# Turning an MLP's results back on VectorE, storing them piece by piece, and dealing out the loads of later pairs: top-k attention and a low-rank mixer on one core

## The chip, the cores and the metric

The kernel runs on one core of a Trainium2 chip. The core has five engines with queues of their own: TensorE (PE: matmuls and transposes, into PSUM), VectorE (DVE), ScalarE (ACT), GpSimd (POOL) and SyncE (SP), which computes nothing and here issues nearly all DMAs. Each engine runs its own instructions strictly in the order in which the kernel wrote them; between engines, semaphores hold back what needs another's result. A DMA is issued by a queue and carried out by 16 DMA engines; the issuing queue goes on to its next instruction when the issue is done, but if that instruction has to wait, all that stands behind it waits too.

The metric is the time of one execution in microseconds (us), lower is better. All data is float32 (the weights arrive as float64, read as pairs of 32-bit words).

## What is computed

```python
# attention: q, k, v are (8, 8, 576, 64): batch, heads, rows, width
scores = (1 / sqrt(64)) * q @ k.transpose(0, 1, 3, 2)
kth = np.partition(scores, -32, axis=-1)[..., -32:-31]
scores = np.where(scores >= kth, scores, -1e9)
attn = np.exp(scores - scores.max(-1, keepdims=True))
attn = attn / (attn.sum(-1, keepdims=True) + 1e-9)
x = (attn @ v).transpose(0, 2, 1, 3).reshape(8, 576, 512)
# mixer: U (576, 32), V (32, 576), w_ch1 (512, 2048), w_ch2 (2048, 512)
h = x.transpose(0, 2, 1) @ U @ V
u = x + h.transpose(0, 2, 1)
out = u + np.maximum(u @ w_ch1, 0) @ w_ch2
```

For each of 64 heads and each of 576 rows the 32 largest scores are kept, weighed and multiplied with v. The mixer joins the heads of a batch, adds a product of rank 32 along the rows, and ends with an MLP whose result is added to its input.

## The kernel before

**Pairs, steps, batches.** Two heads make a pair (`g`, 32 of them), four pairs a batch (`NPAIR` = 4). A pair is worked off in five steps (`CH`): four tiles of 128 rows, both heads side by side, and a last tile `t` = 4 with the 64 rows that are left of both heads. The main loop (L782) runs over `n` = 5 g + t. It is software-pipelined by hand: in step n the scores of tile n+1 are computed, the top-k of tile n runs, tile n-1 is weighed, turned and sent away, and tile n-3 is multiplied with v. The order of all five engines is the order of this text; no scheduler moves anything.

**A tile.** `scores` (L313) multiplies q and k on TensorE, ScalarE copies the result to SBUF (L351). From pair 5 on (`blocked`) the top-k works on folded rows: GpSimd and VectorE split each row into the larger and the smaller of two halves (`pair`, L390 to L393), and VectorE finds the 32nd largest score by `max` and `match_replace` (`front`, L432 to L463). ScalarE and GpSimd push down what is below it (L488, L491), ScalarE takes the exponential (L397). VectorE is needed in every tile for the whole of the top-k.

**Weights to the other side.** The product with v needs the weights transposed. From step 30 on (`ROUNDED`, `shared`) the four large tiles of a pair go round through DRAM: VectorE transposes blocks of 32 x 32 into `y`, which has one buffer (`blocks`, L518), SyncE stores it in four DMAs to `away` (L524) and loads it again as `PT` in one (L528), which first has to wait for those four. `values` (L585) multiplies PT with v, a little more than one step later. The fifth tile, and all before step 30, are transposed on TensorE (`turns`).

**Loads.** `load(g)` brings q, k and v of pair g. A blocked pair takes 16 DMAs of q and k in pieces of 32 columns (L247 with 64 KB, L252 with 8 KB), then five of v (L276 to L280). All 21 are written one after the other at the beginning of step t = 0 of the pair in front (L786), to be turned by VectorE (`prep`, L293) in step t = 1. The tile `ld` has one buffer; the tiles of v have three.

**The MLP as filler.** When a batch's four pairs are mixed (`mixed`), `mlp(b)` is added to `fillers`: a generator that writes one matmul at a time. `fill` is called several times in a step and takes as many of them as are `due`. A batch's MLP runs in two parts: 320 columns (two tiles and the last 64 rows), then 256. In each, 16 tiles of the hidden layer (L656, then ReLU, L668) are followed by four result tiles `c` (L675, 16 matmuls each). A finished result is copied by ScalarE (L690), and GpSimd adds u (L691, into `oT`, two buffers); in the last batch VectorE does both (L688).

**The way out.** `oT` holds the result with its columns on the partitions and must be turned back. In batches 0 to 6, `turned_back` does it on TensorE: two or three transposes (L723), one or two copies by ScalarE (L725, L727) into `ob` (two buffers), and one or two stores (L729, L734). This is written some matmuls behind the result: at f = 12 of the next result tile (L682), at f = 4 of the next part (L669), or at the end of the MLP (L694). In the last batch, but for its very last tile, VectorE turns blocks of 32 x 32 (L705), and eight or twelve stores of 16 or 8 KB follow at once (L710, L715).

Of the kernel before, what the change touches and what calls it, by code (L numbers as in the profile page):

```python
# [26 lines left out]
def kernel(  # L27
# [28 lines left out]
    nc = tc.nc  # L56
# [179 lines left out]
    inverted = set()  # L236

    def load(g):
        b, h0 = g // NPAIR, 2 * (g % NPAIR)
        ld = loads.tile([P, 2 * S], F32, tag="ld", name="ld")  # L240
        if blocked(g):
            for i, src in enumerate((q, k)):
                for a in range(4):
                    ds = src[b, h0 + a // 2, :, a % 2 * BLK : (a % 2 + 1) * BLK]
                    to = ld[a * BLK : (a + 1) * BLK, i * S : (i + 1) * S]
                    lead = TAIL if i and a >= 2 else 0
                    nc.sync.dma_start(  # L247
                        to[:, lead : lead + MAIN].rearrange("i (t m d) -> i t m d", t=NT, d=BLK),
                        ds[0:MAIN].rearrange("(m i t) d -> i t m d", i=BLK, t=NT),
                    )  # L250
                    end = 0 if lead else MAIN
                    nc.sync.dma_start(  # L252
                        to[:, end : end + TAIL].rearrange("i (m d) -> i m d", d=BLK),
                        ds[MAIN:S].rearrange("(m i) d -> i m d", i=BLK),
                    )
            raw[g] = ld
        else:
            tiles = []
            ends = ld[:, 2 * MAIN : 2 * S].rearrange("p (h d) -> p h d", h=2)
            for j, src in enumerate((q, k)):  # L260
                t = ld[:, j * MAIN : (j + 1) * MAIN].rearrange("p (t h d) -> p t h d", t=NT, h=2)
                for i in range(2):
                    queue = nc.scalar if g == 0 and i else nc.sync
                    queue.dma_start(
                        t[:, :, i, :],
                        src[b, h0 + i, 0:MAIN, :].rearrange("(p t) d -> p t d", t=NT),
                    )
                tiles.append(t)
            for i, src in enumerate((q, k)):
                nc.sync.dma_start(  # L270
                    ends[half(i)], src[b, h0 : h0 + 2, MAIN:S, :].rearrange("h p d -> p h d")
                )
            raw[g] = tiles, ends
        va, vd, vt = (a[g % NV] for a in (vas, vds, vts))
        for i in range(2):
            nc.sync.dma_start(  # L276
                va[:, i], v[b, h0 + i, 0:MAIN, :].rearrange("(p t) d -> p t d", t=NT)
            )
            nc.sync.dma_start(vd[half(i), half(i)], v[b, h0 + i, MAIN:S, :])
        nc.sync.dma_start(vt[TAIL:P], v[b, h0 : h0 + 2, MAIN:S, :].rearrange("h p d -> p h d"))  # L280

    def blocked(g):
# [363 lines left out]
    def mlp(b):  # L646

        uT = uTs.pop(b)
        late = []
        for chunks, (lo, hi) in zip(PARTS, SPAN):  # L650
            w = hi - lo
            hTs = []
            for f in range(NF):
                ph = ps_m.tile([P, C], F32, tag="mm", name="mm")
                for cc in range(NC):
                    nc.tensor.matmul(  # L656
                        ph[:, 0:w],
                        lhsT=w1[:, cc, f * P : (f + 1) * P],
                        rhs=uT[:, cc, lo:hi],
                        start=(cc == 0),  # L660
                        stop=(cc == NC - 1),
                    )
                    if cc < NC - 1:
                        yield w / C
                if f % 2 == 0:
                    hT = mlpp.tile([P, 2, WIDE], F32, tag="hT", name="hT", bufs=HT)
                    hTs += [hT[:, 0], hT[:, 1]]
                nc.scalar.activation(hTs[f][:, 0:w], ph[:, 0:w], AF.Relu)  # L668
                if f == 4 and late:  # L669
                    late.pop()()  # L670
                yield w / C
            for c in range(NC):
                po = ps_m.tile([P, C], F32, tag="mm", name="mm")
                for f in range(NF):
                    nc.tensor.matmul(  # L675
                        po[:, 0:w],
                        lhsT=w2[:, f, c * P : (c + 1) * P],
                        rhs=hTs[f][:, 0:w],
                        start=(f == 0),
                        stop=(f == NF - 1),  # L680
                    )
                    if f == 12 and late:  # L682
                        late.pop()()
                    if f < NF - 1:
                        yield w / C
                oT = mlpp.tile([P, WIDE], F32, tag="oT", name="oT")
                if b == B - 1:
                    nc.vector.tensor_tensor(oT[:, 0:w], uT[:, c, lo:hi], po[:, 0:w], ALU.add)  # L688
                else:
                    nc.scalar.copy(oT[:, 0:w], po[:, 0:w])  # L690
                    nc.gpsimd.tensor_tensor(oT[:, 0:w], oT[:, 0:w], uT[:, c, lo:hi], ALU.add)  # L691
                late.append(turned_back(b, chunks, lo, c, oT))
                yield w / C
        late.pop()()  # L694

    def turned_back(b, chunks, lo, c, oT):


        def run():
            cs = slice(c * P, (c + 1) * P)  # L700
            if b == B - 1 and (lo, c) != (SPAN[1][0], NC - 1):

                w = sum(rows(t) for t in chunks)
                ob = mlpp.tile([P, 3 * P], F32, tag="ob", name="ob", bufs=2)
                nc.vector.transpose(ob[:, 0:w], oT[:, 0:w])  # L705
                for a in range(4):
                    cs = slice(c * P + a * BLK, c * P + (a + 1) * BLK)
                    ba = ob[a * BLK : (a + 1) * BLK]
                    for t in chunks[0:2]:
                        nc.sync.dma_start(  # L710
                            out[b, 0:MAIN, cs].rearrange("(m i t) c -> t i m c", i=BLK, t=NT)[t],
                            ba[:, OFF[t] - lo : OFF[t] - lo + P].rearrange("i (m c) -> i m c", c=BLK),
                        )
                    if NT in chunks:
                        nc.sync.dma_start(  # L715
                            out[b, MAIN:S, cs].rearrange("(m i) c -> i m c", i=BLK),
                            ba[:, 2 * P : 2 * P + TAIL].rearrange("i (m c) -> i m c", c=BLK),
                        )
                return
            tp = ps_t.tile([P, 3, P], F32, tag="tp", name="tp")  # L720
            for i, t in enumerate(chunks):
                n = rows(t)
                nc.tensor.transpose(tp[0:n, i, :], oT[:, OFF[t] - lo : OFF[t] - lo + n], ident)  # L723
            ob = mlpp.tile([P, 3, P], F32, tag="ob", name="ob", bufs=2)
            nc.scalar.copy(ob[:, 0:2], tp[:, 0:2, :])  # L725
            if NT in chunks:
                nc.scalar.copy(ob[0:TAIL, 2], tp[0:TAIL, 2, :])  # L727
            t = chunks[0]
            nc.sync.dma_start(  # L729
                out[b, 0:MAIN, cs].rearrange("(p t) c -> p t c", t=NT)[:, t : t + 2, :],  # L730
                ob[:, 0:2],
            )
            if NT in chunks:
                nc.sync.dma_start(out[b, MAIN:S, cs], ob[0:TAIL, 2])  # L734

        return run

    MLP_WORK = 2 * NF * NC * S / C

# [5 lines left out]
    share = MLP_WORK / (NPAIR * SLOTS * (NT + SHORT))  # L745
    fillers, mixing, due = [], [], 0.0

    def fill(k=1):


        nonlocal due
        for _ in range(k):
            if passes:
                passes.pop(0)()
            if mixing and next(mixing[0], True):
                mixing.pop(0)
            due += share * (SHORT if t == NT else 1) * (EARLY if n <= 2 * ALONE + 2 else 1)
            while due > 0:
                if not fillers:
                    due = 0.0  # L760
                    break
                done = next(fillers[0], None)
                if done is None:
                    fillers.pop(0)
                else:
                    due -= done
# [4 lines left out]
        if m % CH == NT:  # L771
            mixing.append(mixed(m // CH, 5, 1 if m < STEPS - 1 else 0))

    load(0)
    next_params(1)
    t = 0
    for _ in prep(0):
# [4 lines left out]
    for n in range(STEPS + 2):  # L782
        g, t = divmod(n, CH)
        if n < STEPS:
            if t == 0 and g + 1 < NP:
                load(g + 1)  # L786
            if t == 1 and g + 1 < NP:
                ready = prep(g + 1)
            fronts[n] = front(g, t)
            next(fronts[n])  # L790
# [107 lines left out]
        fill(2)  # L898
    while mixing or fillers:
        fill()  # L900


# [29 lines left out]
```

## Time and profile before

Three runs took 1718.66, 1716.7 and 1718.15 us: a median of 1718.15. The profiled execution took 1716.65 us, and its span, from the first instruction to the last, is 1714.9 us.

| Engine | busy us | share of the span | instructions |
|---|---|---|---|
| TensorE, matmuls | 1613.5 | 94% | 9489 |
| TensorE, weight loads | 1219.8 | 71% | 9489 |
| VectorE | 1484.2 | 87% | 4317 |
| ScalarE | 1023.3 | 60% | 2582 |
| GpSimd | 944.9 | 55% | 749 |

| Group | number | mean of one |
|---|---|---|
| L723 transposes on TensorE | 142 | 276 ns (128 rows), 272 ns (64) |
| L725 and L727 copies by ScalarE | 57 and 28 | 372 and 258 ns |
| L691 additions by GpSimd, 320 and 256 columns | 28 and 28 | 868 and 731 ns |
| L705 block transposes on VectorE, 320 and 256 columns | 4 and 3 | 512 and 445 ns |
| L518 block transposes of the weights on VectorE | 208 | 682 ns |
| L524 stores to `away` | 416 | 434 ns to issue (median), 2.4 us to land |
| L528 loads of PT | 104 | 338 ns to issue, 3.3 us to land |
| L247 and L252 loads of q and k | 216 each | about 590 and 625 ns to issue, 2.4 and 2.0 us to land |
| L710 stores of pieces in the last batch | 56 | 430 ns to issue, 1.5 us to land |

Matmuls overlap in TensorE, so the mean duration of one is not its price: the chain of waits shows how fast they follow each other (0.11 us for a transpose, 0.22 us for each of the two records that a matmul of 256 columns leaves, 0.27 us for 320). The share of busy time is an average over stages: until 200 us attention runs without an MLP, at 1550 us attention is over, and the rest is the last MLP on TensorE alone. The granted clock is 0.97 over the span, and 1.00 from 440 us on but for the last bit. A DMA's issue occupies SyncE's queue and is not counted as busy. "A <- B" in a list of waits says that A stood until B was done.

### The profile page before, as it was taken

To read this page: it belongs to the slowest core of one execution; us is meant where nothing else is said; L and a number is where in the kernel's file an instruction comes from. 1 tells how busy PE (TensorE), PEld (TensorE's weight loads), DVE (VectorE), ACT (ScalarE), POOL (GpSimd) and SP (SyncE) were. 2 spreads that over 40 slices of the span, in tenths; PEclk is the share of its full clock that TensorE was granted. 3 is DMA by queue.
4 is the path that set the end of the run, shared out by engine and by line. 5 is a ranking of instruction groups with operands and counts; after the bars stand their busy time and mean duration, and the time that the engine had idled before them with its cause. 6 is when DMAs were issued, how large, how long until landed. Compare 5 with 4: busy or idle time off the path is not lost.

```text
span 1714.9 us, 29637 instructions
## 1 busy us (share of the span) xinstructions
PE 1613.5 (94%) x9489; PEld 1219.8 (71%) x9489; DVE 1484.2 (87%) x4317; ACT 1023.3 (60%) x2582; POOL 944.9 (55%) x749
## 2 busy tenths in 40 slices
PE   4666799998999999999999999999999999999999
PEld 2444566787777877788677877788677877788777
DVE  7999989999999999999999999999999999992000
ACT  4888797665656556565656566565655566563100
POOL 4778578666555555565555555565555555552000
PEclk7777899999999999999999999999999999999999
DMA  3322322344444444444444444444444444432010
GB/s 87 95 84 84 84 78 61 77 123 122 108 112 112 117 117 106 112 116 114 115 109 111 119 112 108 114 113 114 111 108 120 118 108 114 106 93 71 3 16 13
DMA packets 275837, 167.37 MB, mean 98 GB/s; under 512 B 173920, under 2 KB 260192, under 8 KB 275680
## 3 DMA queue, kind: packets, MB, share of 16 engines
q1 hardware_dynamic: 274624, 165.20, 37.2%
q8 instruction: 75, 1.23, 0.3%
q14 instruction: 82, 0.67, 0.1%
q10 hardware_dynamic: 1056, 0.26, 0.1%
HBM read 101.42 MB, written 63.96 MB: 96 GB/s over the span
## 4 chain that ended last, share of the span: by engine, by line
PE 71%; DVE 19%; SPq 3%; ACT 2%; issue 2%; DMA 2%; POOL 1%; POOLq 0%; DVEq 0%; ACTq 0%
PE mm L656 27%; PE mm L675 21%; PE sc L323 8%; DVE upper L458 6%; PE O L585 6%; DVE m L463 6%; DVE first L446 2%; SPq L252 2%; PE tp L551 1%; PE O L571 1%; SPq L247 1%; PE up L631 1%; PE O L581 1%; PE tp L546 1%; DVE y L518 1%
## 5 line engine op out<-in xcount | busy, mean ns | idle before, releaser
L675 PE MATMUL mm<-hT,w 128*128 128x256 f32 (+1 forms) x2048 | 529.5, 407 | 0.0
L656 PE MATMUL mm<-uT,w 128*128 128x256 f32 (+1 forms) x2048 | 522.8, 407 | 0.0
L491 POOL TENSOR_TENSOR Ssb<-Ssb,E 128x576 f32<-128x576 f32 x271 | 379.2, 1417 | 246.2 <-ACT E L488 245.8
L656 PEld LDWEIGHTS mm<-uT,w 128*128 128x128 f32 x2048 | 380.0, 191 | 97.6 <-issue 2.6
L675 PEld LDWEIGHTS mm<-hT,w 128*128 128x128 f32 x2048 | 377.9, 191 | 93.0 <-issue 2.9
L463 DVE MAX8 m<-upper 128x8 f32<-128x304 f32 (+1 forms) x864 | 407.7, 508 | 3.6
L458 DVE MATCH_REPLACE8 upper<-m,upper 128x304 f32<-128x304 f32 (+1 forms) x576 | 285.7, 502 | 0.0
L390 POOL TENSOR_TENSOR lower<-Ssb 128x576 uint32<-128x576 uint32 (+1 forms) x135 | 174.3, 1291 | 147.2 <-ACT Ssb L351 51.0
L393 POOL TENSOR_TENSOR lower<-lower,upper 128x576 uint32<-128x576 uint32 (+1 forms) x135 | 174.3, 1291 | 112.2 <-DVE upper L392 104.7
L397 ACT ACTIVATE Ssb<-Ssb,nmax 128x576 f32<-128x576 f32 x286 | 221.5, 777 | 15.3 <-POOL Ssb L468 9.3
L668 ACT ACTIVATE hT<-mm 128x320 f32<-128x320 f32 (+1 forms) x256 | 105.1, 410 | 192.9 <-PE mm L656 191.0
L323 PE MATMUL sc<-qkT 64*128 64x288 f32 x1334 | 211.7, 441 | 8.6 <-ACT Ssb L358 7.8
L488 ACT ACTIVATE E<-Ssb,least 128x576 f32<-128x576 f32 x271 | 198.0, 769 | 5.2
L323 PEld LDWEIGHTS sc<-qkT 64*128 64x128 f32 x1334 | 116.3, 183 | 63.8 <-issue 24.2
L585 PE MATMUL O<-PT,va 128*64 128x128 f32 x2048 | 144.5, 285 | 3.3 <-DMA PT<-away 3.2
L518 DVE STREAM_TRANSPOSE y<-Ssb 128x512 f32<-128x512 f32 x208 | 134.5, 682 | 14.8 <-ACT Ssb L397 14.7
L351 ACT COPY Ssb<-sc 128x576 f32<-128x576 f32 x216 | 127.5, 643 | 32.6 <-PE sc L323 31.0
L688 DVE TENSOR_TENSOR oT<-uT,mm 128x320 f32<-128x320 f32 (+1 forms) x8 | 3.6, 454 | 144.5 <-PE mm L675 144.5
L585 PEld LDWEIGHTS O<-PT,va 128*64 128x64 f32 x2048 | 113.2, 140 | 19.7 <-DMA PT<-away 3.9
L432 DVE MAX8 upper<-lower 128x8 f32<-128x288 f32 x243 | 97.9, 439 | 23.2 <-POOL lower L393 21.2
L392 DVE TENSOR_TENSOR upper<-sc,Ssb 128x576 f32<-128x576 f32 (+1 forms) x135 | 92.0, 682 | 20.7 <-ACT Ssb L351 20.1
L458 DVE MATCH_REPLACE8 upper<-first,upper 128x304 f32<-128x304 f32 x243 | 109.8, 458 | 0.0
(91 smaller groups left out, 1878.7 us busy)
## 6 DMA issues: line engine op xcount, KB each, us to landing
away<-y SPq DMA_DIRECT2D x416, 128.0 KB, 2.4
PT<-away SPq DMA_DIRECT2D x104, 512.0 KB, 3.3
raw<-in_moe_w_ch_dram SPq DMA_DIRECT2D x32, 512.0 KB, 3.9
va<-in_v_dram SPq DMA_DIRECT2D x64, 128.0 KB, 2.2
out_dram<-ob SPq DMA_DIRECT2D x57, 128.0 KB, 2.0
ld<-in_q_dram SPq DMA_DIRECT2D x108, 64.0 KB, 2.6
ld<-in_k_dram SPq DMA_DIRECT2D x108, 64.0 KB, 2.3
ld<-in_q_dram SPq DMA_DIRECT2D x108, 8.0 KB, 2.2
```

The lines of the kernel that those rows point to most:

```text
L323: nc.tensor.matmul(out, lhsT=qkT[half(h), 0, cols(t)], rhs=qkT[half(h), 1, lo:hi], start=True, stop=True,)
L390: nc.gpsimd.tensor_tensor(bottom, a.bitcast(U32), b.bitcast(U32), ALU.add)
L393: nc.gpsimd.tensor_tensor(bottom, bottom, top.bitcast(U32), ALU.subtract)
L397: nc.scalar.activation(E, chunk, AF.Exp, bias=nmax, scale=SCALE, accum_out=total)
L458: nc.vector.match_replace(nxt, ms[c], curs[c], NEG)
L463: nc.vector.max(ms[c], curs[c])
L488: nc.scalar.activation(gap, chunks[c], AF.Relu, bias=least[:, c : c + 1], scale=-WIDEN)
L491: nc.gpsimd.tensor_tensor(chunks[c], chunks[c], gap, ALU.subtract)
L518: nc.vector.transpose(y[:, :, h].rearrange("p r c j -> p c r j"), E2[:, a : a + MAIN].rearrange("p (c r j) -> p c r j", c=NT, r=4),)
L585: nc.tensor.matmul(O[half(h)], lhsT=va[:, h, j, :], rhs=PB[:, h, j] if shared(g, t) else PT[:, NT * h + j], start=False, stop=(j == NT - 1),)
L656: nc.tensor.matmul(ph[:, 0:w], lhsT=w1[:, cc, f * P : (f + 1) * P], rhs=uT[:, cc, lo:hi], start=(cc == 0), stop=(cc == NC - 1),)
L675: nc.tensor.matmul(po[:, 0:w], lhsT=w2[:, f, c * P : (c + 1) * P], rhs=hTs[f][:, 0:w], start=(f == 0), stop=(f == NF - 1),)
```

## The change

Three things change.

1. The result tiles of all batches but the very last tile are turned by VectorE and leave in pieces of 32 columns. `turn_back` is no longer written at a place in the MLP's loop but by a post: `later(6, ...)` puts it on a list with the count of MLP matmuls (`ticks`) at which it is due, and `tick()`, called after every MLP matmul, writes at most one due post.
2. In batches 0 to 6 each piece's store is a post of its own, due 1, 2, 3, ... matmuls after the transpose: twelve for the wider part (eight of 16 KB, four of 8 KB), eight for the other. In the last batch they are written at once, as before.
3. `load` becomes a generator with a `yield` behind each DMA but the last. Up to pair 5 it is run through at step t = 0 of the pair in front, as before. From pair 6 on it is started two pairs ahead, in step t = 2 (`coming`), and every `fill` writes one DMA of it; what is left is written in step t = 1, before `prep`.

```diff
-                if f == 4 and late:
-                    late.pop()()
...
-                    if f == 12 and late:
-                        late.pop()()
+                    tick()
...
-                late.append(turned_back(b, chunks, lo, c, oT))
+                later(6, lambda a=(b, chunks, lo, c, oT): turn_back(*a))
...
+    def turn_back(b, chunks, lo, c, oT):
+        cs = slice(c * P, (c + 1) * P)
+        if (b, lo, c) != (B - 1, SPAN[1][0], NC - 1):
+            w = sum(rows(t) for t in chunks)
+            ob = mlpp.tile([P, 3 * P], F32, tag="ob", name="ob", bufs=2)
+            nc.vector.transpose(ob[:, 0:w], oT[:, 0:w])
+            wait = 0
+            for a in range(4):
...
+                for to, piece in pieces:
+                    if b == B - 1:
+                        nc.sync.dma_start(to, piece)
+                    else:
+                        wait += 1
+                        later(wait, lambda to=to, piece=piece: nc.sync.dma_start(to, piece))
+            return
...
+    posts, ticks = [], 0
+    def later(wait, job):
+        at = ticks + wait
+        i = sum(p[0] <= at for p in posts)
+        posts.insert(i, (at, job))
+    def tick():
+        nonlocal ticks
+        ticks += 1
+        if posts and posts[0][0] <= ticks:
+            posts.pop(0)[1]()
+    coming = []
+    def send():
+        if coming and next(coming[0], True):
+            coming.pop(0)
     def fill(k=1):
...
             if passes:
                 passes.pop(0)()
+            send()
...
-            if t == 0 and g + 1 < NP:
-                load(g + 1)
+            if t == 0 and g <= NPAIR:
+                for _ in load(g + 1):
+                    pass
+            if t == 2 and NPAIR <= g < NP - 2:
+                coming.append(load(g + 2))
             if t == 1 and g + 1 < NP:
+                while coming:
+                    send()
                 ready = prep(g + 1)
...
     while mixing or fillers:
         fill()
+    while posts:
+        tick()
```

## The prediction

> **What bounds the kernel now.** I read first the busy time by stretch (columns: stretch, its length, then busy us and instructions of TensorE, its weight loads, VectorE, ScalarE, GpSimd, then clock, DMA share, GB/s):
>
> ```profile
> 300.00:440.00 140.00, 133.69 (x839) 104.99 (x838) 134.88 (x418) 86.36 (x225) 84.18 (x67) 0.98 0.42 106
> ...
> 700.00:800.00 100.00, 100.00 (x616) 79.71 (x615) 95.75 (x292) 60.40 (x161) 58.12 (x46) 1.00 0.44 114
> 800.00:900.00 100.00, 98.73 (x578) 72.05 (x576) 94.21 (x289) 61.38 (x154) 57.26 (x46) 1.00 0.45 114
> ```
>
> From about 440 to 1550 us TensorE is never idle but for one wait that returns in each batch, VectorE stands 4 to 6 us per 100 behind it, and after 1556 TensorE works alone at the last MLP. The chain of waits agrees: 71% TensorE, 19% VectorE. The wait that returns, and who sits on SyncE's queue, are in the waits (us in total, times, longest):
>
> ```profile
> PE tp L723 <- POOL oT L691: 9.8, 7, 2.1
> ...
> SPq L528 <- DMA away<-y: 205.9, 212, 3.1
> ```
>
> The first is the product stream standing before a result's turn-back (L723) until GpSimd has added u (7 times, 9.8 us). In the list of one line's waits the same stall comes at 818.4, 1012.2, 1205.9 and 1399.7, so the kernel repeats every 193.8 us, a batch of four pairs. The second says that SyncE's queue stands still about 2 us per attention tile, because the load of PT must wait until the four "away" stores have landed.
>
> That queue is what I read last, over one pair. Here are its last two tiles, and the beginning of the next pair's loads (start, duration):
>
> ```profile
> 724.36 1.75 SPq L524 DMA_DIRECT2D away<-y  x4
> 728.17 0.34 SPq L528 DMA_DIRECT2D PT<-away  x1
> 728.55 0.44 SPq L729 DMA_DIRECT2D out_dram<-ob  x1
> 729.03 0.48 SPq L734 DMA_DIRECT2D out_dram<-ob  x1
> 733.00 1.77 SPq L524 DMA_DIRECT2D away<-y  x4
> 737.08 0.34 SPq L528 DMA_DIRECT2D PT<-away  x1
> 737.46 0.66 SPq L247 DMA_DIRECT2D ld<-in_q_dram  x1
> 738.17 0.62 SPq L252 DMA_DIRECT2D ld<-in_q_dram  x1
> 738.83 0.64 SPq L247 DMA_DIRECT2D ld<-in_q_dram  x1
> ```
>
> A tile holds the queue for 4.2 us (four issues, the wait, PT's issue; 3.8 to PT's issue). An issued load holds it 0.65 us with its gap. Tiles t1, t2, t3 of a pair come 8 to 12 us apart, then the one-headed tile 4 makes no away and the gap to the next t0 is 18 to 20 us: the burst of 21 loads lies there. How much room PT has: its issue plus the 3.3 us that its DMAs take to land, against the matmul that reads it.
>
> ```profile
> 743.82 0.38 PE L581 MATMUL O<-PT,vd 128*128 128x128 f32 x2
> 744.14 1.09 PE L585 MATMUL O<-PT,va 128*64 128x128 f32 x16
> ```
>
> PT issued at 737.08 has landed at 740.4 and is read at 744.1: 3.7 us to spare. Over all tiles from 440 to 1500 the margin goes from about 1.2 us (some t2) to 7 us (t1). It is short, and nothing on TensorE can pass a late PT.
>
> **Part 1, the turn-back leaves TensorE and ScalarE.** Of 142 transposes of L723 two stay. In the chain three take 0.33 us and two 0.22, so 0.11 each: 140 x 0.11 = 15.4 us, 2.2 a batch. The 9.8 us of waits for oT go too, bar the last 0.5. ScalarE loses 56 copies of L725 and 28 of L727 (372 and 258 ns: 28 us), worth nothing in itself, as it is 60% busy. So the gain is at most 15.4 + 9.3 = 24.7 us, if nothing else comes late.
>
> **Part 2, VectorE gets 56 transposes.** The same operation in the last batch takes 512 ns (320 columns) and 445 ns (256): 28 x 0.512 + 28 x 0.445 = 26.8 us, 3.8 a batch. VectorE is busy 95.0 of 100 us, 184.1 of 193.8: with 3.8 it is 187.9, and some 1.5 us of idle time in a batch are issue gaps and not waits, so it needs at least 189.4. It still fits under TensorE (192.5 busy - 2.2 = 190.3), with 1 us to spare. The transposes also wait for oT, and behind them stand the top-k and y. I set the VectorE instruction ahead of each in the new order beside GpSimd's end of L691 in the old trace: in a steady batch five are late enough to wait for nothing, three would wait 1.0, 1.5 and 1.2 us if taken alone. Taken in order each delay hides the next, and about 0.5 us is left. VectorE's present waits (y L518 2.8 us, scores L392 0.8 to 1.7) are their cover; were it gone, 3.7 us a batch. Bounds: 0 to 3.7, I take 0.5.
>
> **Part 3, SyncE's queue.** 84 stores (56 of 128 KB, 28 of 32) become 560 of 16 or 8 KB in seven batches (20 a pair on average, but 48 in the first half of a batch's MLP and 32 in the second, so two pairs of four get all). In the last batch twelve such stores were issued from 1630.81 to 1636.57: 0.48 us each. And the 21 loads (16 at 0.65, 5 of v in 2.9 us: 13.3 us) leave the wide gap: by the new order of instructions six stand ahead of t1's away, eight ahead of t2's, seven ahead of t3's, where tiles are 8 to 12 us apart. The queue is strictly in order, so all of them count.
>
> The pair with the larger stores, from y of t0 ready at 703.1 (end of L518): four tiles 3 x 4.2 + 3.8 = 16.4; loads 13.3; stores between them 9 + 8 + 8 = 25, 12.0; landing 3.3. Sum 45.0, so t3's PT is there at 748.1, where L585 now reads it at 744.1: **+4.0 us**. The 1.3 us of transposes that TensorE saves here are lost in that wait.
>
> The pair with the smaller stores (8 + 6 + 7). y of t0 ready at 799.4 + 1.4 (two transposes of 0.445, 0.5 of waiting) = 800.8; tile 4.2, 6 loads 3.9, 8 stores 3.8: 812.7, just past y of t1 (810.5 + 1.9); tile 4.2, 8 loads 5.2, 6 stores 2.9: 825.0; tile 4.2, loads 4.2, 7 stores 3.4: 836.8; 3.8 + 3.3: 843.9, against 841.6 now: **+2.3 us**; TensorE alone would be at 839.5.
>
> Do these add up? VectorE waits for scores (L392) at 681.4 and at 777.9 with no margin, and between L585 of t3 and that wait TensorE is saturated without a transpose to lose: a late TensorE makes VectorE as late. One more transpose (0.5) lies between the second wait and the next large pair. So a batch costs 4.0 + 2.3 + 0.5 = **6.8 us**, and five batches (487 to 1456 us) have both pairs: 34.
>
> The first batch's stores fall in 326 to 440, where VectorE bounds. Queue free at 326.4; 6 loads 3.9 + 11 stores 5.3; tile 4.2; 8 loads 5.2 + 11 stores 5.3; 3.8 + 3.3: 357.4, and VectorE's own transposes about 1: 358.4 against 350.4, **+8**. VectorE can't make it up: its y of t3 (one buffer) waits for that late away. The last batch has no loads left to deal, and its second half runs after VectorE is done: -1.3 - 0.9 - 1.3, with 1 us of VectorE lateness, **-2.5**.
>
> Sum: 1716.65 us (span 1714.9 and 1.75 around it) + 34 + 8 - 2.5 = 1756.2. The runs' median is 1.5 above the profiled execution: 1757.7, **1758**.
>
> Bounds of what is not in the trace: an issue in a mixed stream of loads and stores. From below: the shortest L252 took 0.32 us and L710 0.315; from above: a burst has one issue of 1.4 to 1.7 us now and then (L247 up to 1.47). With only the large pair's delay, 4.0 + 0.5 less the 2.2 that TensorE then keeps of its relief in the small one, so 2.3 a batch: 1735; without the first batch's 8 too: 1727. With 0.32 for every issue it is the first rival. With issues 20% dearer: 46 x 0.11 + 42 x 0.11 = 9.7 a batch, about +48. DMA time is no bound: share 0.44 now.
>
> The Trainium skill speaks against this reckoning: "DMA: Bandwidth & Descriptors", section "Issuing engines are not separate DMA queues", holds the time that a sequencer takes to initiate a DMA to be usually small beside the DMA itself. In this trace a small store's issue has 0.43 of 1.5 us, and 21 loads hold the queue 13 us. By the rule Part 3 would cost near nothing and the sum would be that of the first rival.
>
> **Rivals.** (1) Faster: the queue keeps up, and TensorE bounds as before: 1718.15 - 24.7 + 0.5 for VectorE = 1694. For it: SyncE's queue waits 270.2 + 90.6 us for y, 14 a pair of the 26. The point: 46 issues in the large pair must fit in 41.0 - 1.3 - 16.4 - 3.3 = 20.0 us, 0.44 each; I count 0.55. Chance 0.08. (2) VectorE becomes the pace, with the queue no bound: 189.4 + 3.7 = 193.1 a batch where 193.8 was, -0.7 x 6, the end -2.5: 1711. Against it: its waits hide in those that it has. Chance 0.05. (3) The queue collapses: long issues in every tile, or late aways holding the one y buffer in all pairs, so 16 us or more a batch: 1800 and above. Against it: the two pairs without stores have only 0.6 to 1.3 us of lateness with 2 or more to spare. Chance 0.07. The forecast 0.8, 1725 to 1795 by the bounds above. Between them, no change: 0.02, where 0.2% is about what a measurement of this kernel can tell. So slower 0.86, faster 0.12, same 0.02.
>
> **What would show it.** Right: "PE O L585 <- DMA PT<-away" among TensorE's longest waits, some 5 to 7 us a batch in two pairs of four, with the issues of stores and loads unbroken on SyncE's queue ahead of the late away; period about 200.6 us; no L723 but two; VectorE's L703 waiting under 1 us. Wrong: TensorE full from 440 to 1550 and a period under 193, or VectorE without gaps while PT is early.

## The result, and the profile after

The changed kernel takes 1788.26 us (median of 4 runs, 1787.18 to 1790.66), the kernel before took 1717.67 beside it (4 runs, 1716.7 to 1718.66): a ratio of 1.0413, 95% interval 1.0395 to 1.0431. It is slower by some 71 us. The profiled execution has a span of 1788.8 us against 1714.9, so the difference to explain in the traces is 73.9 (the profiled execution is the slowest of the four). The lines of the file have moved by a few: L590 is the product that was L585, L523 the turning y (L518), L529 and L533 away and PT's load (L524, L528), L249 and L255 loads of q and k (L247, L252), L328 the scores (L323). L703 is now VectorE's turn-back and L725 the small stores.

First the page: busy time of each engine (share of the span, instructions), the shares of the chain that ended last, and one of the costliest groups (busy us, mean ns of one, then the idle time before it and what ended it):

```profile
PE 1633.7 (91%) x9349; PEld 1230.1 (69%) x9349; DVE 1508.5 (84%) x4373; ACT 1002.3 (56%) x2498; POOL 944.8 (53%) x749
...
PE 59%; DVE 20%; DMA 8%; SPq 4%; ACT 4%; POOL 3%; issue 2%; DVEq 0%; POOLq 0%; ACTq 0%
...
L590 PE MATMUL O<-PT,va 128*64 128x128 f32 x2048 | 155.8, 300 | 65.8 <-DMA PT<-away 65.5
```

The same group on the page of the kernel before:

```profile
L585 PE MATMUL O<-PT,va 128*64 128x128 f32 x2048 | 144.5, 285 | 3.3 <-DMA PT<-away 3.2
```

Read two things. TensorE now stands 65.5 us before products whose PT has not landed (3.2 before the change), and the chain has 12% of DMA and SyncE's queue in it (5% before). And TensorE is busy for longer, 1633.7 us against 1613.5, although it does 140 transposes fewer. The span splits into these two: TensorE's idle time went from 101.4 (1714.9 - 1613.5) to 155.1 us, +53.7, its busy time +20.2. The transposes that left were worth 15.4, so the same work as before has become 35.6 us slower. The mean granted clock, 0.970 before, is 0.944.

The waits of the whole run, VectorE's turn-back in the steady part (500 to 1500 us) last (us in total, times, longest):

```profile
PE O L590 <- DMA PT<-away: 65.5, 23, 5.6
...
DVE y L523 <- DMA away<-y: 34.8, 11, 4.8
...
DVE ob L703 <- POOL oT L693: 2.0, 5, 0.4
```

Late are PT and, in the same queue, the away that keeps the one y buffer. The turn-back on VectorE itself waits for next to nothing there.

SyncE's queue ahead of one late PT (start, duration), a pair with the large stores, from PT of t1 to PT of t2:

```profile
750.31 0.34 SPq L533 DMA_DIRECT2D PT<-away  x1
750.70 0.61 SPq L249 DMA_DIRECT2D ld<-in_q_dram  x1
751.37 0.62 SPq L725 DMA_DIRECT2D out_dram<-ob  x1
...
753.44 1.69 SPq L249 DMA_DIRECT2D ld<-in_k_dram  x1
...
760.84 1.83 SPq L529 DMA_DIRECT2D away<-y  x4
764.68 0.34 SPq L533 DMA_DIRECT2D PT<-away  x1
```

Between the two PTs the queue never rests: eight loads and eight stores take it from 750.70 to 760.84, 10.1 us, where the prediction counted 5.2 + 3.8 = 9.0 (one of the loads took 1.69 us to issue). Only then come the four aways, their landing and PT. In the list of starts, 46 such issues of the pair took 26.8 us, 0.58 each.

And TensorE at the same place (in square brackets: idle before, and what ended it):

```profile
763.41 0.38 PE L586 MATMUL O<-PT,vd 128*128 128x128 f32 x2
768.49 1.97 PE L590 MATMUL O<-PT,va 128*64 128x128 f32 x16 [4.69 <-DMA PT<-away]
770.39 2.29 PE L328 MATMUL sc<-qkT 64*128 64x288 f32 x8
```

The stall ends 3.8 us after PT's issue. Then look at the durations behind it: 16 products take 1.97 us, where 16 of them took 1.09 in the prediction's lines, and the eight scores take 2.29, where eight behind no stall took 1.24 in this trace (at 679.34). Busy time by stretch around a stall of the other kind of pair shows the clock itself (stretch, length, busy us and instructions of TensorE, weight loads, VectorE, ScalarE, GpSimd, then clock, DMA share, GB/s); PT landed here at 666.26, after a wait of 4.45 us:

```profile
653.00:661.00 8.00, 8.00 (x48) 5.64 (x48) 6.47 (x17) 6.51 (x17) 5.59 (x4) 1.00 0.40 72
661.00:666.30 5.30, 0.85 (x7) 0.50 (x5) 3.65 (x11) 0.35 (x1) 1.40 (x1) 0.80 0.62 170
666.30:671.00 4.70, 4.70 (x26) 3.33 (x27) 3.96 (x14) 1.39 (x3) 0.00 (x0) 0.50 0.35 79
671.00:679.00 8.00, 7.88 (x40) 5.63 (x41) 7.20 (x24) 4.75 (x13) 4.54 (x4) 1.00 0.47 135
```

The clock, at 1.00 in the 8 us before, falls to half during the stall, stays there for 4.7 us of work, and is full again. If it is only ever full or half, as in all nine traces, 0.80 over the 5.3 us of the stall is 2.1 us at half, so 6.8 us in all; the 4.7 that are spent working lose 2.35 us. A late PT costs its wait and that.

The same stall comes at 666.26, 870.30 and 1075.93: a batch takes 204.8 us, where it took 193.8. Setting the moments at which PT is issued and read beside those of the trace before gives the course of the loss: none until 337 us, 19.6 at 466 (the first batch's stores), then 58.3 more by 1483, and 4.0 won back in the rest: 73.9. In the steady part each pair with a late PT moves the products by about 7 us, once by 10 (4 to 5 of wait, 2.3 of clock, up to 0.8 for the next PT), and the tiles up to the next such pair win back 1.0 or 2.4 of it.

### The profile page after: what moved, and what is told of

It is laid out like the page before. It is cut to its first block, busy times and chain, and to the rows that moved or that the text cites. A ratio compares the mean times of both kernels' runs of the same rounds, so it can differ in the third digit from the quotient of the medians.

```text
span 1788.8 us, 29787 instructions
## 1 busy us (share of the span) xinstructions
PE 1633.7 (91%) x9349; PEld 1230.1 (69%) x9349; DVE 1508.5 (84%) x4373; ACT 1002.3 (56%) x2498; POOL 944.8 (53%) x749
## 4 chain that ended last, share of the span: by engine, by line
PE 59%; DVE 20%; DMA 8%; SPq 4%; ACT 4%; POOL 3%; issue 2%; DVEq 0%; POOLq 0%; ACTq 0%
PE mm L678 21%; PE mm L660 18%; PE sc L328 7%; DVE upper L463 6%; DVE m L468 6%; PE O L590 5%; DMA PT<-away 4%; DMA away<-y 3%; DVE first L451 2%; SPq L725 2%; PE O L576 2%; DVE y L523 2%; SPq L529 1%; PE up L636 1%; PE tp L556 1%
## 5 line engine op out<-in xcount | busy, mean ns | idle before, releaser
L660 PEld LDWEIGHTS mm<-uT,w 128*128 128x128 f32 x2048 | 385.4, 193 | 99.7 <-issue 3.9
L328 PE MATMUL sc<-qkT 64*128 64x288 f32 x1334 | 226.4, 465 | 8.9 <-ACT Ssb L363 7.9
L590 PE MATMUL O<-PT,va 128*64 128x128 f32 x2048 | 155.8, 300 | 65.8 <-DMA PT<-away 65.5
L590 PEld LDWEIGHTS O<-PT,va 128*64 128x64 f32 x2048 | 122.5, 149 | 84.0 <-DMA PT<-away 70.9
L523 DVE STREAM_TRANSPOSE y<-Ssb 128x512 f32<-128x512 f32 x208 | 136.2, 687 | 44.2 <-DMA away<-y 34.8
L328 PEld LDWEIGHTS sc<-qkT 64*128 64x128 f32 x1334 | 123.3, 195 | 69.0 <-issue 25.6
L599 ACT COPY XT<-O 128x128 f32<-128x128 f32 x128 | 34.0, 266 | 211.9 <-PE O L590 211.8
```

Source lines behind the costliest of these rows:

```text
L328: nc.tensor.matmul(out, lhsT=qkT[half(h), 0, cols(t)], rhs=qkT[half(h), 1, lo:hi], start=True, stop=True,)
L523: nc.vector.transpose(y[:, :, h].rearrange("p r c j -> p c r j"), E2[:, a : a + MAIN].rearrange("p (c r j) -> p c r j", c=NT, r=4),)
L590: nc.tensor.matmul(O[half(h)], lhsT=va[:, h, j, :], rhs=PB[:, h, j] if shared(g, t) else PT[:, NT * h + j], start=False, stop=(j == NT - 1),)
L660: nc.tensor.matmul(ph[:, 0:w], lhsT=w1[:, cc, f * P : (f + 1) * P], rhs=uT[:, cc, lo:hi], start=(cc == 0), stop=(cc == NC - 1),)
```

## The experiments

Three questions: is it the loads or the stores on SyncE's queue, or only both together; is it the number of issues, the stores' bytes, or VectorE's new work; and what does a stall of TensorE cost beyond its length?

**Loads back in one burst (loads_in_burst).** The changed kernel, with the loads issued at a pair's t0 in all pairs; the stores stay among the products.

```diff
-            if t == 0 and g <= NPAIR:
+            if t == 0 and g + 1 < NP:
                 for _ in load(g + 1):
                     pass
-            if t == 2 and NPAIR <= g < NP - 2:
-                coming.append(load(g + 2))
```

> Only the loads go back: all 21 of a pair at once in step t = 0, as before; VectorE still turns the results and their pieces still go out one by one. Theory A (SyncE's queue is too full between t0 and t3 only because loads AND stores stand there): in the pair with the larger stores 16.4 + 12.0 + 3.3 = 31.7 us, under the 41 that there are, so PT is never late after the first batch, TensorE's clock stays at 1.00, and the 15.4 us of transposes and 9 of waits come out: about 1696 to 1706. Theory B (VectorE's 56 transposes and their waits for oT are the cost): still 1760 or more, with VectorE without gaps. Theory C (560 small stores alone overfill the queue or the DMA engines): 1740 or more, PT late in the same two pairs.

Measured: 1716.29 us (10 runs, 1713.33 to 1720.05), ratio 0.9991 (0.9982 to 1.0001). Nearly all of the loss is gone, but the kernel is not faster than before, so the expectation missed its size. TensorE's waits for PT are still 17.8 us (14 times, the longest 2.4). SyncE's queue, behind a burst, says where from:

```profile
949.46 0.51 SPq L283 DMA_DIRECT2D vd<-in_v_dram  x1
...
950.74 5.76 SPq L725 DMA_DIRECT2D out_dram<-ob  x12
956.60 1.81 SPq L529 DMA_DIRECT2D away<-y  x4
960.51 0.34 SPq L533 DMA_DIRECT2D PT<-away  x1
```

The burst ran from 936.08 on; the stores that fell due meanwhile stand behind it, and the 5.76 us of twelve stores push t0's away to 956.60. The wide gap of 18 to 20 us, which held the burst alone, is overfull by about 2 us: one PT a batch comes late (1.96 us at 770.15, 1.97 at 963.87, 1.40 at 1158.09, 2.04 at 1351.44), and the period from one of these to the next is the old one, 193.8. So the queue's room is the question in the wide gap too.

**The dealing of the loads alone (loads_dealt_alone).** The kernel before, with the loads dealt out as in the change; results and stores as before.

```diff
-            if t == 0 and g + 1 < NP:
-                load(g + 1)
+            if t == 0 and g <= NPAIR:
+                for _ in load(g + 1):
+                    pass
+            if t == 2 and NPAIR <= g < NP - 2:
+                coming.append(load(g + 2))
```

> The kernel before, with its transposes on TensorE and its few large stores, and only the loads dealt out over the steps of the pairs in front. Theory A: t0 to t3 hold 16.4 + 13.3 + some 2 us of large stores + 3.3 = 35 us of 41, so late aways of about 1 us, no late PT in a steady batch, time within 6 us of before (1712 to 1724). If the dealt loads alone are the cost: PT late in all four pairs, 1745 or more.

Measured: 1718.13 us (10 runs), ratio 1.0006 (0.9996 to 1.0015). As expected, no change: from 440 us on the products that read PT stay within 0.1 to 0.5 us of the trace before. PT itself is issued up to 3.4 us later (740.45 for 737.08), which the room that it had takes up. Without the small stores the narrow gaps have room for the loads.

**Stores issued by ScalarE (stores_on_scalar_queue).** The changed kernel, with the small stores of batches 0 to 6 on the other issuing engine.

```diff
-                        later(wait, lambda to=to, piece=piece: nc.sync.dma_start(to, piece))
+                        later(wait, lambda to=to, piece=piece: nc.scalar.dma_start(to, piece))
```

> The changed kernel, with loads dealt, but the small stores of batches 0 to 6 issued by ScalarE's queue instead of SyncE's. All DMAs, bytes and VectorE's work are the same. Theory A (issue time on one in-order queue): SyncE's queue has room, no late PT, 1695 to 1725; ScalarE pays 560 x 0.45 = 252 us of queue, 36 a batch, on 113 busy of 194, so it may be late here and there. Theory C' (small DMAs slow the landing of away and PT, or the DMA engines are full): as slow as the change, 1780 or more.

Measured: 1777.6 us (4 runs, 1772.52 to 1778.42), ratio 1.034 (1.0325 to 1.0356). A miss, and one that decides nothing, because the edit brought a wait of its own. The waits of SyncE's queue:

```profile
SPq L529 <- DMA out_dram<-ob: 99.4, 33, 26.1
...
SPq L533 <- DMA out_dram<-ob: 49.4, 16, 5.0
```

SyncE's aways now stand 99.4 us, once 26.1, for stores of the other queue to land, and TensorE stands 56.1 us before late PTs again. In the built program the DMAs of both queues take the same eight completion semaphores (counters that a DMA raises when it has landed) in turn, so an away waits for the store that had its semaphore before it, and ScalarE, in order behind its own work, issues that store late. The trace names the semaphore of each wait and bears this out: an away stands from 718.29 to 724.76 for number 104, which is the number of a store that ScalarE issued at 723.36 and that landed at 724.76. No run with separate semaphores was made.

**Stores left out (stores_left_out).** The changed kernel, loads dealt, results turned on VectorE.

```diff
-                        wait += 1
-                        later(wait, lambda to=to, piece=piece: nc.sync.dma_start(to, piece))
+                        pass
```

> The changed kernel without the stores of batches 0 to 6 (seven eighths of the output are not written); VectorE turns every result as in the change, loads are dealt. Theory A (the issues of stores and loads together overfill SyncE's queue between t0 and t3): 16.4 + 13.3 + 3.3 = 33 us of 41, no late PT in a steady batch, clock 1.00, VectorE's 26.8 us of transposes hidden: 1692 to 1705. Theory B (VectorE's transposes and waits are what costs): 1740 or more.

Measured: 1700.88 us (4 runs), ratio 0.9903 (0.9888 to 0.9918), as expected. TensorE's waits for PT are down to 7.7 us (7 times). A stretch of the steady part:

```profile
700.00:900.00 200.00, 200.00 (x1191) 152.41 (x1190) 196.62 (x600) 121.69 (x309) 118.25 (x94) 1.00 0.42 106
```

TensorE is busy for 200.00 of 200 us at full clock, VectorE for 196.62. So VectorE has room for the transposes, and TensorE gets its relief, as soon as no small stores stand in the queue. On its page TensorE's busy time is 1599.0 us for the same 9349 instructions that took 1633.7 in the changed kernel: 34.7 us of slower clock, counted in another way than the 35.6 above.

**Half the bytes (half_the_bytes).** The changed kernel; every small store of batches 0 to 6 carries half its rows, the number of issues is the same.

```diff
-  ... nc.sync.dma_start(to, piece))
+  ... nc.sync.dma_start(to[:, 0 : to.shape[1] // 2], piece[:, 0 : to.shape[1] // 2]))
```

> The changed kernel with as many stores at the same places, each with the first half of its rows (half of the output of batches 0 to 6 is not written). Theory A (number of issues in order on one queue): a store of 8 KB is issued in 0.43 us where one of 16 KB took 0.43 to 0.45, so nothing is gained: 1775 to 1795. Theory C' (bytes and 128 B packets crowd the DMA engines and make away and PT land late): about half of the loss comes back, 1740 to 1760.

Measured: 1789.0 us (4 runs, 1783.87 to 1791.92), ratio 1.0414 (1.039 to 1.0438), with 61.8 us of TensorE's waits for PT (24 times, the longest 5.2). As expected, the changed kernel's time: it is not what the stores carry. Their issues are as many as before, and they stand in the same places of the queue.

**What a stall costs (stalls_by_length).** The kernel before, with chains of small GpSimd additions on a tile `zed` and one transpose of it by TensorE at seven places of the last MLP, where TensorE works alone: seven stalls of chosen length.

```diff
+    def stall(src, links):
+        nc.gpsimd.tensor_tensor(zed, src[:, 0:P], ident, ALU.add)
+        for _ in range(links):
+            nc.gpsimd.tensor_tensor(zed, zed, ident, ALU.add)
+        tp = ps_t.tile([P, P], F32, tag="tp", name="st")
+        nc.tensor.transpose(tp, zed, ident)
```

> The kernel before, with seven stalls of TensorE put into the last MLP, where it works alone: a transpose that waits for a chain of 1 to 15 GpSimd additions, so idle for about 1.5, 2.4, 3.3, 3.8 us in the wider part and 4.7, 5.6, 8 us in the other. The result is unchanged; the time has the stalls in it. Theory (a stall over some 2.5 us makes the granted clock fall to 0.5 for some us, which is what the sum lacked): the short ones cost their length, the longer ones 2 to 3.4 us more, with a stretch of clock 0.50 after each. Rival (the clock fell in the changed kernel for another reason, such as load): clock 1.00 after every one of them.

Measured: 1762.76 us (one run). On TensorE's timeline L654 is the transpose that ends a stall; the L688 behind it are products, 64 of 320 columns each time:

```profile
1624.02 0.33 PE L654 MATMUL st<-ident,zed 128*128 128x128 f32 x1 [2.12 <-POOL zed L652]
...
1626.34 17.39 PE L688 MATMUL mm<-hT,w 128*128 128x320 f32 x64
1647.03 0.48 PE L654 MATMUL st<-ident,zed 128*128 128x128 f32 x1 [3.31 <-POOL zed L652]
1647.30 20.13 PE L688 MATMUL mm<-hT,w 128*128 128x320 f32 x64
```

Sixty-four products take 17.39 us after a stall of 2.12 us (and after one of 1.06), and 20.13 after one of 3.31: 2.7 more. Measured in the same way, stalls of 3.84, 4.78, 5.84 and 8.55 us cost 2.6, 2.9, 1.6 and 2.2 us beyond their length, each with the granted clock at 0.50 for 6.8 us (10.2 at the longest). So in this place the price is a step between 2.1 and 3.3 us, some 2 to 3 us high, and not a share of the stall; that is the theory's forecast, but for the 1.6. How high the step is follows from the clock. TensorE's work at half clock, after the stalls of 3.31 and 5.84 us:

```profile
1647.03:1652.82 5.79, 5.79 (x12) 3.83 (x13) 0.00 (x0) 0.00 (x0) 0.00 (x0) 0.50 0.14 21
1714.09:1717.67 3.58, 3.58 (x9) 2.95 (x10) 0.00 (x0) 0.00 (x0) 0.00 (x0) 0.50 0.00 0
```

Half of that, 2.9 and 1.8 us, is close to the price found (2.7 and 1.6, and 0.15 for the slower transpose); after 3.84, 4.78 and 8.55 us it is half of 5.44, 6.06 and 4.72. The longer stalls cost less because more of the time at half clock lies within the stall.

Where a stall falls decides too. In all nine traces the granted clock is 0.50 or 1.00 and changes only on a grid of 3.41 us, whatever the kernel does; call one piece of the grid a slot. Two stalls in the trace of loads_in_burst, each as the slot in which TensorE is idle longest and the slot behind it:

```profile
961.57:964.98 3.41, 1.44 (x21) 1.11 (x21) 3.41 (x13) 0.14 (x1) 2.01 (x2) 1.00 0.84 257
964.98:968.39 3.41, 3.41 (x15) 2.22 (x16) 3.41 (x13) 1.07 (x3) 0.52 (x1) 0.50 0.48 141
...
575.90:579.31 3.41, 1.64 (x22) 1.30 (x24) 3.41 (x14) 0.27 (x1) 1.39 (x2) 1.00 0.88 271
579.31:582.70 3.39, 3.39 (x23) 2.88 (x20) 3.39 (x14) 2.32 (x6) 1.09 (x2) 1.00 0.43 120
```

The first stall, 1.97 us, lies in one slot, and the next slot is at half clock. The second is longer, 2.40 us, but two slots share it, the larger part is 1.8, and the clock stays. Over the nine traces, 4176 slots at full clock have a slot behind them: none of the 3951 with less than 1.3 us of idle TensorE was followed by half clock, and all 103 with more than 2.1 us were; between these, both occur. Half clock did not end behind a slot with more than 0.55 us of idle time (179 of them), so a stall that reaches far enough into a second slot costs two. This is counted in the traces; no run moved one stall along the grid on purpose.

The Trainium skill ("TensorE: Matmul & The Clock Gate", section "What's actually happening") has the array at half clock after an idle window of about 3.4 us, and back after about as long a busy one, the windows running free. The traces agree on a length of 3.41 us and on windows that run free. They differ on what it takes: an idle time of 3.31 us, and even of 1.97, is shorter than such a window and halved the clock.

**Stores spread to where the queue is free (stores_spread).** A version meant to win: loads in the burst; batch 0 turned back on TensorE as in the kernel before; from batch 1 on VectorE turns, and the stores leave from their own list only in steps t2, t3 and t4, at a set pace per product of the MLP; ob has five buffers, three of them idle tiles named raw.

```diff
+    PACE = {2: 0.9, 3: 0.62, 4: 0.6}
...
-                        later(wait, lambda to=to, piece=piece: nc.sync.dma_start(to, piece))
+                        stores.append(lambda to=to, piece=piece: nc.sync.dma_start(to, piece))
...
+        elif stores:
+            room[0] += PACE.get(t, 0.0) if n < STEPS else 1.0
+            if room[0] >= 1:
+                room[0] -= 1
+                stores.pop(0)()
```

> Loads in one burst at t = 0 as before; the first batch is turned back on TensorE as before; in batches 1 to 6 VectorE turns back, and the stores wait on a list of their own that is only emptied in steps t = 2, 3, 4 (at most some 11, 11 and 6 between two tiles), with five buffers for ob. Theory A: no interval of SyncE's queue is over its time (t3 to t0: 13.6 of 14.5 us, the others up to 5.3 beside 4.2 of 9 to 11), so PT is in time, TensorE is the pace with 190.3 us a batch and six batches give 20 us: 1696 to 1704. If VectorE, at 189.9 of 190.3, slips behind: 1705 to 1714. If small stores cost beyond their issue: 1716 or more.

Measured: 1698.0 us (4 runs, 1697.55 to 1698.28), ratio to the kernel before 0.9884 (0.9869 to 0.9898), as expected: it beats both. TensorE waits 7.4 us for PT. SyncE's queue over two tiles:

```profile
703.25 0.34 SPq L533 DMA_DIRECT2D PT<-away  x1
703.64 3.74 SPq L731 DMA_DIRECT2D out_dram<-raw  x8
710.88 1.76 SPq L529 DMA_DIRECT2D away<-y  x4
```

Eight stores go out in 3.74 us, and the queue is free again 3.5 us before the next away. Batches 1 to 6 still issue 480 of the 560 small stores. Among dealt loads the stores cost 87 us (1788.26 against 1700.88 without them); where they have the narrow gaps to themselves, they cost nothing that shows. (The first batch is turned on TensorE here, so the two figures are not for quite the same work.)

## Why the prediction was right, and where its size was off

It had the right cause and side, and 1788 lies in its range; its own figure, 1758, was 30 us short. That the range still holds it is in part luck: its upper part was argued from issues 20% dearer, and an issue was 6% dearer (0.583 for 0.55 us). What filled it was a cost that the sum does not have, the clock.

**The mechanism** was Part 3's: dealt loads and small stores together overfill SyncE's queue between t0 and t3 of the two pairs with stores. It is shown by taking either away: with the loads in a burst 1716.29, with the stores left out 1700.88, with the loads dealt and the old stores 1718.13, and with both 1788. That the bytes do not count is shown by half_the_bytes, and that most of the same issues cost nothing in gaps of their own by stores_spread.

**Part 1** was right: the relief is there, but only where the queue lets TensorE have it (1700.88 and 1698.0). In the changed kernel it went into the waits for PT.

**Part 2** was right: 2.0 us of waits at L703 in five batches, against 0.5 a batch and a bound of 3.7. Only in the first batch may VectorE's work show: behind it the products are still 5.0 us late with the stores left out, and 4.8 with the loads in a burst, where "about 1" was counted. How much of that is VectorE's work and how much the slower clock behind a stall of 3.8 us there was not separated.

**Part 3's issues and waits** were nearly right. In the large pair shown an issue took 0.58 us for 0.55 counted, and a landing 3.8 for 3.3. From y of t0 to PT of t3 in the large pair the trace has 43.4 us, the prediction 41.7. The wait falls mainly on t2's PT and not on t3's, since the mixed issues weigh most there, but its length is the one worked out: in the large pair TensorE was to stand for 4.0 + 1.3 = 5.3 us, and stood 4.8 to 6.0 (5.3 on average over five batches); in the small pair 2.3 + 2.15 = 4.45 (with the transposes it no longer has), and stood 3.9 to 5.6 (4.5 on average). The sign named for it, waits of 5 to 7 us a batch, is less than this sum and was too small; they were near 10. Over the whole run the prediction lengthens the span by 34 + 8 - 2.5 = 39.5 while TensorE does 15.4 us less, so it implies 54.9 us more of idle time: 53.7 were measured.

**The term that was mis-sized** is the 6.8 us a batch, and the first batch's 8 with it: they count TensorE at full clock behind a late PT. A stall of 4 to 5 us also halves the clock for 4.7 us of work, 2.3 us each time: two a batch make 4.6, and 6.8 + 4.6 = 11.4, where 11.0 were measured. Over the run the clock took 35.6 us, and 39.5 + 35.6 = 75.1 against 73.9. In the first batch 19.6 were lost for the 8, of which some 5 stay without the stores (above): from 300 to 440 us TensorE's idle time grew by 10.8 (from 6.3 to 17.1), the implied 8 + 2.2, and the granted clock there is 0.93 where it was 0.98. The last batch won back 4.0, not 2.5. The trace before had shown both sides. Its five waits of 1.27 us left the clock at 1.00, but a wait of 2.14 us for oT that ends at 422.14 was followed by this stretch, and it is what makes the 0.98 in the first row of the prediction:

```profile
423.07:429.90 6.83, 5.91 (x31) 4.26 (x32) 6.83 (x21) 3.28 (x9) 3.81 (x3) 0.50 0.38 97
```

**The rivals.** The first needed 0.44 us an issue, and the issue took 0.58. The second made VectorE the pace, at 1711; with the queue relieved the kernel runs at 1700.88 with TensorE full, so it isn't. The third wanted 16 us or more a batch; 11.0 came, though the clock brought the total within 12 us of it. The skill's sentence that was weighed there ("DMA: Bandwidth & Descriptors", that the time to initiate a DMA is usually small beside the DMA) is no guide to the price here: an issue of a small store had 0.43 of 1.5 us in the trace before, halving the stores' bytes changed nothing, and leaving the stores out took 87 us away (1788.26 to 1700.88). What counts is the sum of the issues on one queue, stretch by stretch.

**Still open.** Why single issues take 1.1 to 1.9 us now and then; what decides whether a slot with 1.3 to 2.1 us of idle time is followed by half clock; and what the 5 us in the first batch are made of.

## What to carry to other kernels

Count the issues of an in-order DMA queue between two transfers that something waits for, stretch by stretch and with everything that the edit moves there: two parts that each fit may not fit together. When the count gives a stall of TensorE where it bounds the kernel, price its length and half of the working time that falls into half clock behind it, and look in the trace for a stall of that length and the clock that followed. Many small stores can be had for nothing if they are given the gaps in which the queue stands empty.

## What was not expected of the hardware

The step in the price of a stall: nothing for 2.12 us, 2.7 us for 3.31 us, with the granted clock at half for 6.8 us, and, since the clock changes only every 3.41 us, a price that hangs on where the stall falls (1.97 us halved it, 2.40 us did not). And a second issuing engine did not free the first: with the stores on ScalarE, SyncE's aways waited 99.4 us for them.
